# Top-k attention with an ELU feed-forward: four heads in the step of the last queries, another layout of the last keys, another schedule for the weights' decoding and the feed-forward

## The chip, the core and the metric

The kernel runs on one core of one Trainium2 chip. The metric is the device time in microseconds of one execution; the time before is the median of three runs. The profile is one further execution, recorded by the hardware profiler. Engines are named as in the profile: PE (TensorE matmul), PEld (its weight loads), DVE (VectorE), ACT (ScalarE), POOL (GpSimd), SP (the queue that issues the DMAs).

## The reference

Eight batches of eight heads, 576 tokens, 64 dimensions a head. The attention keeps, in every row of scores, those at or above the 32nd largest:

```python
def _attn_ref(q, k, v):
    B, H, S, D = q.shape                      # 8, 8, 576, 64
    scores = np.matmul(q, k.transpose(0, 1, 3, 2)) / np.sqrt(D)
    kth = np.partition(scores, -32, axis=-1)[..., -32:-31]
    scores = np.where(scores >= kth, scores, -1e9)
    attn = np.exp(scores - np.max(scores, axis=-1, keepdims=True))
    attn = attn / (np.sum(attn, axis=-1, keepdims=True) + 1e-9)
    return np.matmul(attn, v)

x = attn_out.transpose(0, 2, 1, 3).reshape(B * S, H * D)     # 4608 x 512
h = x @ w_in                                                # 512 x 2048
g = np.where(h > 0, h, np.exp(np.minimum(h, 0)) - 1)
out = g @ w_out                                             # 2048 x 512
```

The weights arrive as 64-bit floats and are turned into 32-bit floats on the chip. All arithmetic is in 32-bit floats.

## The kernel before

The 576 queries of a batch are four tiles of 128 (`qt` 0 to 3; tile `qt` holds every fourth token) and a rest of 64 (`qt` 4). A **step** is one query tile for one pair of heads `hp`: it computes two score tiles of 128 x 576 (`scores`, L252 and L261), finds the 32 largest of every row for each head (`select`: a MAX8, then three times a MATCH_REPLACE8 and a MAX8, L277, L281 and L287), turns the scores into exponentials that are zero outside the selection (`mask`, L298 to L302), divides by the sum (`normalise`, L309 to L313), transposes the result (`trans` and `trans_rest`, L326 to L342) and, once a group of one or two query tiles is complete, multiplies by V (`attend`, L360). L377 copies the product to `xT`, the transposed input of the feed-forward. In a step of the rest the two heads' 64 rows share the 128 partitions, so one selection serves both (`nh` = 1, `weight` = 0.5). There are 128 full steps and 32 of the rest.

The feed-forward works on **blocks** of one to three slots of 128 tokens. The first pair of batches has blocks of 1, 1, 2, 2 and 3 slots, each of the other three pairs has three blocks of 3: fourteen blocks, 36 slots. The last slot of a pair holds the rests of both batches. A block that has all its columns of `xT` adds its pieces to the list `ffn` (`ffn_pieces`): sixteen `hidden(f)`, each of four matmuls over the 512 inputs (L390), two ACT instructions (L398, L399) and one on DVE that writes `gT` (L400), and then for every slot four `project` pieces of four matmuls (L411), with an eviction (L420) and stores to `out` after the fourth. In the profile every 32-bit matmul is two PE instructions, so a piece of either kind shows as x8; a transpose is one.

Buffers: `sc` 5, `wk` 2, `et` 2, `kv` 5 of each kind, `xT` 2, `gT` 2 halves; in PSUM one tile of four banks for the scores, two banks for transposes, V products (`ps_t`), and two for the feed-forward (`ps_f`). `gT` lives in a pool that is opened only when the last weight is decoded and the raw buffers are given back.

The weights come in 32 pieces (16 of `w_in`, 16 of `w_out`). `hook`, called eight times in a full step between the passes of `select`, decodes one piece: `convert_first` and `convert_last` have three DVE instructions (L151, L154, L164), four on ACT and two on POOL.

The loop runs over the steps. Iteration n writes down the scores of step n+2, the selection of step n, the masking of step n-1 and the transposes of step n-2, and four times calls `feed`, which has a credit of 8 units a step (4 in a step of the rest) and takes pieces from `ffn` while the credit pays for them:

```python
        credit[0] = min(credit[0] + FEED * share * u.weight, 2 * FEED)
        while ffn and credit[0] >= ffn[0][0]:
```

What is left in `ffn` after the loop is written out at its end. The loads and transposes of the next batch's K, Q and V are put at fixed steps ahead of it (`at`). The source order is not the order in which an engine runs its instructions: the framework, which also sets all semaphores, arranges the instructions of each engine when the kernel is built. A tile taken from a pool waits until an older tile of the pool has had its last reader.

Of the kernel before, what the change touches and what calls it, by code (L numbers as in the profile page):

```python
# [16 lines left out]
EPS = 1.0e-9  # L17
STEEP = 1.0e30
FEED = 8.0
# [17 lines left out]
class Block:  # L37


    def __init__(self, slots):  # L40
        self.slots = slots
        self.xT = None
        self.gT = []
        self.left = 0
        self.tiles = [[] for _ in range(slots)]
# [10 lines left out]
class Step:  # L56


    def __init__(self, t, hp, group, at):
        self.t, self.hp = t, hp  # L60
        self.group, self.at = group, at
        self.nh = 1 if t.rem else 2
        self.weight = 0.5 if t.rem else 1.0
# [3 lines left out]
def kernel(  # L67
# [44 lines left out]
    rawpool = raws.enter_context(tc.tile_pool(name="raw", bufs=4))  # L112
# [13 lines left out]
    def weight(i):  # L126
        per = dff // WN
        if i < NC * per:
            c, f = divmod(i, per)
            src = moe_w_in[c * P : (c + 1) * P, 2 * f * WN : 2 * (f + 1) * WN]  # L130
            return src, w_in[:, c, f * WN : (f + 1) * WN]
        f = i - NC * per
        return moe_w_out[f * P : (f + 1) * P, :], w_out[:, f, :]
# [36 lines left out]
    decode = []  # L170

# [9 lines left out]
    def decode_piece(i):  # L181
        if i < 2 * NF:
            if i + 3 < 2 * NF:
                load_weight(i + 3)
            convert_first(i)
        if i > 0:
            convert_last(i - 1)

    loaded, kqT, vT = {}, {}, {}

# [14 lines left out]
    def load_v(b, hp):  # L205
        t = kvpool.tile([P, 2, J + 1, D], FP32, tag="vT", name="vT")
        for hh in range(2):
            h = 2 * hp + hh
            nc.sync.dma_start(
                t[:, hh, 0:J, :],  # L210
                v[b, h, 0:JP, :].rearrange("(p j) d -> p j d", j=J),
            )
        nc.sync.dma_start(
            t[0:R, :, J, :],
            v[b, 2 * hp : 2 * hp + 2, JP:S, :].rearrange("h p d -> p h d"),
        )
        vT[b, hp] = t

    def transpose_qk(b, hp):
        d = kvpool.tile([P, 2, S], FP32, tag="kqT", name="kqT")  # L220
        kqT[b, hp] = d
        srcs = [loaded.pop((b, hp, name)) for name in ("k", "q")]
        for i, src in enumerate(srcs):
            ps = ps_t.tile([P, JP], FP32, tag="t", name="qkps")
            for c in range(J):
                nc.tensor.transpose(
                    ps[:, c * P : (c + 1) * P],
                    src[:, c, :, :].rearrange("p h d -> p (h d)"),
                    ident[:],
                )  # L230
# [8 lines left out]
        nc.scalar.copy(  # L239
            d[:, :, JP:S], ps[:, 0 : 2 * R].rearrange("p (a s) -> p a s", a=2)  # L240
        )

    def scores(u):
        t = u.t
        kq = kqT[t.b, u.hp]
        q0 = t.qt * P
        u.sc = scpool.tile([P, 2, S], FP32, tag="sc", name="sc")
        ps = ps_sc.tile([P, 2, 2, 512], FP32, tag="s", name="scps")
        for half in range(2):
            for i in range(2):  # L250
                rows = slice(i * D, i * D + R) if t.rem else slice(0, P)
                nc.tensor.matmul(  # L252
                    ps[rows, i, half, 0:HS],
                    kq[i * D : (i + 1) * D, 1, q0 : q0 + t.ql],
                    kq[i * D : (i + 1) * D, 0, half * HS : (half + 1) * HS],
                    start=True,
                    stop=True,
                )
        for i in range(2):
            rows = slice(i * D, i * D + R) if t.rem else slice(0, P)  # L260
            nc.scalar.activation(  # L261
                u.sc[rows, 0 if t.rem else i, :].rearrange("p (a s) -> p a s", a=2),
                ps[rows, i, :, 0:HS],
                AF.Copy,
                scale=scale,
            )

    def select(u, i):
        if i >= u.nh:
            return  # L270
# [5 lines left out]
        hook()  # L276
# [3 lines left out]
        for r in range(TOP_K // 8 - 1):  # L280
# [7 lines left out]
            hook()  # L288

    def mask(u, i):  # L290

        if i >= u.nh:
            return
        if i == 0:
            u.den = small.tile([P, 2], FP32, tag="den", name="den")
        sc, low, top = u.sc[:, i, :], u.last[:, i, 7:8], u.first[:, i, 0:1]
# [9 lines left out]
    def normalise(u):  # L306
        nh = u.nh
        den = small.tile([P, 2], FP32, tag="dene", name="dene")
        nc.gpsimd.tensor_scalar_add(den[:, 0:nh], u.den[:, 0:nh], EPS)  # L309
        rec = small.tile([P, 2], FP32, tag="rec", name="rec")  # L310
        nc.vector.reciprocal(rec[:, 0:nh], den[:, 0:nh])  # L311
        for i in range(nh):
# [4 lines left out]
    def trans(u):  # L317

        g = u.group
        if g.et is None:  # L320
            n = len(g.tiles)
            g.et = etpool.tile([P, 2 * J + 2, n, P], FP32, tag="et", name="et")
        for i in range(u.nh):
            ps = ps_t.tile([P, JP], FP32, tag="t", name="eps")
            for c in range(J):
                nc.tensor.transpose(  # L326
                    ps[:, c * P : (c + 1) * P],
                    u.sc[:, i, c * P : (c + 1) * P],
                    ident[:],
                )  # L330
            nc.scalar.copy(  # L331
                g.et[:, i * J : (i + 1) * J, u.at, :],
                ps[:].rearrange("p (c q) -> p c q", c=J),
            )

    def trans_rest(u):

        g = u.group
        ps = ps_t.tile([P, JP], FP32, tag="t", name="eps")
        for i in range(u.nh):  # L340
            nc.tensor.transpose(ps[0:R, i * P : (i + 1) * P], u.sc[:, i, JP:S], ident[:])
        nc.scalar.copy(  # L342
            g.et[0:R, 2 * J : 2 * J + u.nh, u.at, :],
            ps[0:R, 0 : u.nh * P].rearrange("p (c q) -> p c q", c=u.nh),
        )

    def attend(g):
        t, hp = g.tiles[0], g.hp
        et, vt = g.et, vT[t.b, hp]
        n = sum(x.ql for x in g.tiles)  # L350
        ps = ps_t.tile([P, JP], FP32, tag="t", name="avps")
        for c in range(J + 1):
            for i in range(2):
                keys = slice(0, P if c < J else R)
                if t.rem:
                    w = et[keys, 2 * J if c == J else c, 0, i * R : (i + 1) * R]
                else:
                    w = et[keys, 2 * J + i if c == J else i * J + c, :, :]
                    w = w.rearrange("p a q -> p (a q)")
                nc.tensor.matmul(  # L360
                    ps[i * D : (i + 1) * D, 0:n],
                    vt[keys, i, c, :],
                    w,
                    start=(c == 0),
                    stop=(c == J),
                )
        c0 = 0
        tiles = list(g.tiles)
        while tiles:
            blk, lo = tiles[0].block, tiles[0].cols.start  # L370
            c1 = c0
            while tiles and tiles[0].block is blk:
                blk.left -= 1
                c1 += tiles.pop(0).ql
            if blk.xT is None:
                blk.xT = xtpool.tile([P, NC, T], FP32, tag="xT", name="xT")
            nc.scalar.copy(blk.xT[:, hp, lo : lo + c1 - c0], ps[:, c0:c1])  # L377
            c0 = c1
            if blk.left == 0:
                ffn.extend(ffn_pieces(blk))  # L380

    def ffn_pieces(blk):
        n_tok = blk.slots * P

        def hidden(f):
            if f % NG == 0:
                blk.gT.append(late["g"].tile([P, NG, T], FP32, tag="g", name="gT"))
# [18 lines left out]
        def project(s, part):  # L406
# [18 lines left out]
        return [(blk.slots, lambda f=f: hidden(f)) for f in range(NF)] + [  # L425
            (3.8, lambda s=s, part=part: project(s, part))
# [6 lines left out]
    blocks = []  # L433
    for b in range(B):
        if b % 2 == 0:
            sizes = (1, 1, 2, 2, 3) if b == 0 else (3, 3, 3)
            slots = [(x, s) for x in map(Block, sizes) for s in range(x.slots)]
# [15 lines left out]
        for qts in ((0,), (1,), (2, 3), (4,)) if b == 0 else ((0, 1), (2, 3), (4,)):  # L453
            for hp in range(NHP):
# [9 lines left out]
    for b in range(1, B):  # L464
        f = first[b]
        for hp, (ahead, ready, late_v) in enumerate(
            ((12, 9, 8), (9, 5, 0), (6, 4, -1), (5, 3, -2))
# [5 lines left out]
    credit = [0.0]  # L473

    def feed(u, share):

        if "g" not in late:
            return
        credit[0] = min(credit[0] + FEED * share * u.weight, 2 * FEED)
        while ffn and credit[0] >= ffn[0][0]:  # L480
            cost, piece = ffn.pop(0)
            credit[0] -= cost
            piece()

    load_qk(0, 0)
    for i in range(3):
# [18 lines left out]
    closing = []  # L505
    for n in range(NS + 3):
        for fn, args in todo.pop(n, []):
            fn(*args)
        now = steps[min(n, NS - 1)]
# [5 lines left out]
        feed(now, 0.25)  # L515
        if cur:
            select(cur, 0)
        while closing:
            attend(closing.pop())
        feed(now, 0.25)  # L520
        if prev:
            mask(prev, 1)
        if done:
            trans(done)
        feed(now, 0.25)
# [4 lines left out]
        if done:  # L530
            trans_rest(done)
            if done.at == len(done.group.tiles) - 1:
                closing.append(done.group)
        feed(now, 0.25)
    while ffn:
        ffn.pop(0)[1]()
# [33 lines left out]
```

## Time and profile before

| | us |
|---|---|
| median of three runs | 1917.54 (1917.00 to 1917.82) |
| the profiled execution | 1917.18 |
| its span, first to last instruction | 1915.4 |
| PE busy / DVE busy / ACT busy / POOL busy | 1709.2 / 1615.8 / 1169.8 / 447.2 |
| mean granted TensorE clock | 0.948 of full speed |
| PE busy in 48 to 96 us, 96 to 144 us | 0.0, 10.8 |
| last matmul of attention / last matmul | 1815 / 1911 |

A page row of the costliest groups gives line, engine, operation, tiles written and read, shape, count, then busy time, the mean of one in ns, and the engine's idle time just before. Busy time is a union: neighbours that overlap in the pipeline count once, so busy over count is below the mean. In a timeline a row is start, length, engine, line, operation, tiles, shape and count, and in brackets the engine's idle time before it with what ended it.

### The profile page before, as it was taken

To read this page: it belongs to the slowest core of one execution; us is meant where nothing else is said; L and a number is where in the kernel's file an instruction comes from. 1 tells how busy PE (TensorE), PEld (TensorE's weight loads), DVE (VectorE), ACT (ScalarE), POOL (GpSimd) and SP (SyncE) were. 2 spreads that over 40 slices of the span, in tenths; PEclk is the share of its full clock that TensorE was granted. 3 is DMA by queue.
4 is the path that set the end of the run, shared out by engine and by line. 5 is a ranking of instruction groups with operands and counts; after the bars stand their busy time and mean duration, and the time that the engine had idled before them with its cause. 6 is when DMAs were issued, how large, how long until landed. Compare 5 with 4: busy or idle time off the path is not lost.

```text
span 1915.4 us, 24954 instructions
## 1 busy us (share of the span) xinstructions
PE 1709.2 (89%) x7984; PEld 946.7 (49%) x7984; DVE 1615.8 (84%) x3360; ACT 1169.8 (61%) x2453; POOL 447.2 (23%) x1096
## 2 busy tenths in 40 slices
PE   4028999999999999899989999999999999999999
PEld 2015656465554455455454455455555455445553
DVE  7999989999799998996999777997899777999310
ACT  6677667576666776575566466566566566557330
POOL 4774212222122222221222111221122211222000
PEclk7557999999899999999999999999999999999999
DMA  6430011000200110001100010000100000000000
GB/s 175 150 130 3 19 31 32 18 13 19 56 1 12 38 31 19 12 13 43 37 1 6 24 44 19 12 18 19 49 13 0 25 19 19 7 12 1 12 6 17
DMA packets 100610, 56.14 MB, mean 29 GB/s; under 512 B 83584, under 2 KB 91776, under 8 KB 100480
## 3 DMA queue, kind: packets, MB, share of 16 engines
q1 hardware_dynamic: 100480, 54.55, 10.3%
q8 instruction: 64, 1.05, 0.2%
q14 instruction: 66, 0.54, 0.1%
HBM read 45.09 MB, written 9.44 MB: 28 GB/s over the span
## 4 chain that ended last, share of the span: by engine, by line
DVE 56%; PE 31%; ACT 8%; issue 2%; POOL 1%; DMA 1%; SPq 0%; POOLq 0%; ACTq 0%; DVEq 0%
DVE wk L281 22%; DVE m L287 20%; PE hps L390 11%; PE ops L411 8%; DVE m L277 7%; PE scps L252 5%; PE avps L360 3%; DVE gT L400 3%; ACT sc L301 2%; PE eps L326 2%; ACT sc L261 2%; ACT sc L302 1%; DVE raw L164 1%; DVE raw L154 1%; DVE raw L151 1%
## 5 line engine op out<-in xcount | busy, mean ns | idle before, releaser
L287 DVE MAX8 m<-wk 128x8 f32<-128x576 f32 x864 | 631.9, 761 | 4.1
L390 PE MATMUL hps<-xT,w_in 128*128 128x384 f32 (+2 forms) x1792 | 544.5, 451 | 16.3 <-DVE gT L400 15.2
L411 PE MATMUL ops<-w_out,gT 128*128 128x512 f32 x1152 | 534.2, 604 | 0.0
L281 DVE MATCH_REPLACE8 wk<-m,wk 128x576 f32<-128x576 f32 x576 | 432.4, 754 | 0.0
L301 ACT ACTIVATE sc<-sc,neg 128x576 f32<-128x576 f32 x288 | 223.1, 775 | 336.5 <-POOL neg L298 336.0
L390 PEld LDWEIGHTS hps<-xT,w_in 128*128 128x128 f32 x1792 | 310.9, 192 | 196.0 <-DVE gT L400 31.0
L411 PEld LDWEIGHTS ops<-w_out,gT 128*128 128x128 f32 x1152 | 208.7, 192 | 223.1 <-issue 219.1
L252 PE MATMUL scps<-kqT 64*128 64x288 f32 (+1 forms) x1280 | 255.4, 456 | 17.4 <-ACT sc L261 15.8
L298 POOL TENSOR_SCALAR neg<-m 128x1 f32<-128x1 f32 x288 | 62.8, 218 | 847.2 <-DVE m L287 845.9
L277 DVE MAX8 m<-sc 128x8 f32<-128x576 f32 x288 | 215.7, 758 | 51.9 <-ACT sc L261 51.5
L313 POOL TENSOR_SCALAR sc<-sc,rec 128x576 f32<-128x576 f32 x288 | 214.0, 753 | 116.6 <-DVE rec L311 93.3
L302 ACT ACTIVATE sc<-sc,gap 128x576 f32<-128x576 f32 x288 | 223.4, 776 | 15.4 <-ACT sc L301 1.5
L360 PE MATMUL avps<-et,vT 128*64 128x256 f32 (+5 forms) x2000 | 205.9, 342 | 26.3 <-ACT et L342 25.6
L281 DVE MATCH_REPLACE8 wk<-m,sc 128x576 f32<-128x576 f32 x288 | 216.6, 754 | 0.0
L326 PE MATMUL eps<-ident,sc 128*128 128x128 f32 x1152 | 173.2, 284 | 48.1 <-ACT xT L377 23.5
L261 ACT ACTIVATE sc<-scps 128x576 f32<-128x576 f32 (+1 forms) x320 | 192.6, 641 | 28.9 <-PE scps L252 27.7
L400 DVE SCALAR_TENSOR_TENSOR gT<-n,hps 128x384 f32<-128x384 f32 (+2 forms) x224 | 109.9, 491 | 116.7 <-ACT n L399 115.0
L326 PEld LDWEIGHTS eps<-ident,sc 128*128 128x128 f32 x1152 | 133.4, 145 | 124.5 <-issue 70.7
L331 ACT COPY et<-eps 128x512 f32<-128x512 f32 x288 | 159.9, 585 | 51.4 <-PE eps L326 50.5
L360 PEld LDWEIGHTS avps<-et,vT 128*64 128x64 f32 (+1 forms) x2000 | 113.7, 141 | 135.2 <-issue 48.2
L252 PEld LDWEIGHTS scps<-kqT 64*128 64x128 f32 (+1 forms) x1280 | 121.0, 186 | 104.3 <-issue 58.2
L398 ACT ACTIVATE n<-hps 128x384 f32<-128x384 f32 (+2 forms) x224 | 98.3, 439 | 119.7 <-PE hps L390 118.1
(41 smaller groups left out, 969.1 us busy)
## 6 DMA issues: line engine op xcount, KB each, us to landing
kin<-in_k_dram SPq DMA_DIRECT2D x64, 128.0 KB, 2.7
qin<-in_q_dram SPq DMA_DIRECT2D x64, 128.0 KB, 2.8
raw<-in_moe_w_in_dram SPq DMA_DIRECT2D x16, 512.0 KB, 4.6
vT<-in_v_dram SPq DMA_DIRECT2D x64, 128.0 KB, 2.1
raw<-in_moe_w_out_dram SPq DMA_DIRECT2D x16, 512.0 KB, 3.2
out_dram<-osb SPq DMA_DIRECT2D x32, 256.0 KB, 2.3
kin<-in_k_dram SPq DMA_DIRECT2D x32, 32.0 KB, 2.5
qin<-in_q_dram SPq DMA_DIRECT2D x32, 32.0 KB, 2.5
```

The costliest lines, as they stand in the source:

```text
L252: nc.tensor.matmul(ps[rows, i, half, 0:HS], kq[i * D : (i + 1) * D, 1, q0 : q0 + t.ql], kq[i * D : (i + 1) * D, 0, half * HS : (half + 1) ...
L261: nc.scalar.activation(u.sc[rows, 0 if t.rem else i, :].rearrange("p (a s) -> p a s", a=2), ps[rows, i, :, 0:HS], AF.Copy, scale=scale,)
L277: nc.vector.max(m, sc)
L281: nc.vector.match_replace(wk[:], m, cur, TAKEN)
L287: nc.vector.max(m, cur)
L301: nc.scalar.activation(sc, sc, AF.Prelu, bias=neg[:], alpha=STEEP)
L302: nc.scalar.activation(sc, sc, AF.Exp, bias=gap[:], accum_out=u.den[:, i : i + 1])
L313: nc.gpsimd.tensor_scalar(u.sc[:, i, :], u.sc[:, i, :], rec[:, i : i + 1], 1.0, ALU.mult, ALU.mult)
L326: nc.tensor.transpose(ps[:, c * P : (c + 1) * P], u.sc[:, i, c * P : (c + 1) * P], ident[:],)
L360: nc.tensor.matmul(ps[i * D : (i + 1) * D, 0:n], vt[keys, i, c, :], w, start=(c == 0), stop=(c == J),)
L390: nc.tensor.matmul(ps[:, 0:n_tok], w_in[:, i, f * P : (f + 1) * P], blk.xT[:, i, 0:n_tok], start=(i == 0), stop=(i == NC - 1),)
L411: nc.tensor.matmul(blk.o[:], blk.gT[f // NG][:, f % NG, s * P : (s + 1) * P], w_out[:, f, :], start=(f == 0), stop=(f == NF - 1),)
```

## The change

- A step of the rest now takes the last queries of **four** heads (two on each half of the partitions, two selections): 16 such steps in place of 32. `weight` and `nh` go. `attend` serves two head pairs in such a group.
- The scores of a head are two matmuls, of 512 and of 64 keys. Head 1's 64 last keys stand ahead of its others in `sc`, so that both heads' last keys are side by side and the transposes go in nine chunks of 128 (`turn`: four, one and four) instead of eight and two halves. V's last keys lie on partitions 0 to 63 for one head and 64 to 127 for the other, with a DMA each.
- `hook` is called twice in a selection instead of four times. The raw buffers are three (before: four), and a pool `early` holds the `gT` of block 0. `w_in` is decoded by columns first.
- In the first eight steps the masking, division and transposes are written one iteration earlier.
- `feed` compares a running sum of TensorE time, spent by attention and feed-forward, with a budget of 12.4 us a step, and asks of every piece that enough weight pieces are decoded.
- The loads and transposes of the next batch stand at other steps.

The core of the diff:

```diff
-FEED = 8.0
+PACE = 12.4
...
     def __init__(self, t, hp, group, at):
-        self.nh = 1 if t.rem else 2
-        self.weight = 0.5 if t.rem else 1.0
+        self.masked = self.normal = self.turned = False
+        if t.rem:
+            rows = [(4 * hp, 0), (4 * hp + 2, 0), (4 * hp + 3, 1), (4 * hp + 1, 1)]
+            self.heads = [
+                (h, i, slice(64 * (n % 2), 64 * (n % 2) + 64))
+                for n, (h, i) in enumerate(rows)
+            ]
+        else:
+            self.heads = [(2 * hp + i, i, slice(0, 128)) for i in range(2)]
...
-    rawpool = raws.enter_context(tc.tile_pool(name="raw", bufs=4))
+    early = raws.enter_context(tc.tile_pool(name="early", bufs=1))
+    rawpool = raws.enter_context(tc.tile_pool(name="raw", bufs=3))
...
-            c, f = divmod(i, per)
+            f, c = divmod(i, NC)
...
+    decoded = [0]
...
     def decode_piece(i):
         if i < 2 * NF:
-            if i + 3 < 2 * NF:
-                load_weight(i + 3)
+            if i + 2 < 2 * NF:
+                load_weight(i + 2)
             convert_first(i)
         if i > 0:
             convert_last(i - 1)
+            decoded[0] = i
...
     def scores(u):
+        first = (0, 3 * JP - R)
+        main = (0, 3 * JP)
+        rest = (JP, 3 * JP - R)
+        for start, keys in ((main, slice(0, JP)), (rest, slice(JP, S))):
+            for h, i, rows in u.heads:
+                kq = kqT[u.t.b, h // 2]
+                part = slice(i * D, (i + 1) * D)
                 nc.tensor.matmul(
+                    ps[rows, start[i] : start[i] + keys.stop - keys.start],
+                    kq[part, 1, q0 : q0 + u.t.ql],
+                    kq[part, 0, keys],
...
+        spent(1.2)
...
     def select(u, i):
-        hook()
         nc.vector.max(m, sc)
...
             nc.vector.max(m, cur)
-            hook()
+            if r != 1:
+                hook()
...
+    def turn(u, chunks):
...
+        sc = u.sc[:, :, :].rearrange("p i s -> p (i s)")
+        for c in range(n):
+            c0 = (chunks.start + c) * P
+            nc.tensor.transpose(ps[:, c * P : (c + 1) * P], sc[:, c0 : c0 + P], ident[:])
+        spent(0.115 * n)
...
         def hidden(f):
-            if f % NG == 0:
-                blk.gT.append(late["g"].tile([P, NG, T], FP32, tag="g", name="gT"))
+            if f == 0 and blk.number == 0:
+                g = early.tile([P, NF, P], FP32, tag="g", name="gT")
+                blk.gT = [g[:, 0:NG], g[:, NG:NF]]
+            elif f % NG == 0 and blk.number > 0:
+                g = late["g"].tile([P, NG, T], FP32, tag="g", name="gT")
+                blk.gT.append(g[:])
...
-        return [(blk.slots, lambda f=f: hidden(f)) for f in range(NF)] + [
-            (3.8, lambda s=s, part=part: project(s, part))
+        part = {1: 1.15, 2: 1.85, 3: 2.7}[blk.slots]
+        behind = 2 * NF + 1 if blk.number else 0
+        return [
+            (part, max(behind, NC * (f // 4 + 1)), lambda f=f: hidden(f))
+            for f in range(NF)
+        ] + [
+            (3.55, max(behind, NF + (part + 1) * NF // 4),
+             lambda s=s, part=part: project(s, part))
             for s in range(blk.slots)
             for part in range(4)
         ]
...
-            for hp in range(NHP):
+            for hp in range(NHP // 2 if qts == (4,) else NHP):
...
-            ((12, 9, 8), (9, 5, 0), (6, 4, -1), (5, 3, -2))
+            ((8, 6, 5), (6, 4, 0), (4, 3, -1), (3, 2, -2))
...
-        if "g" not in late:
-            return
-        credit[0] = min(credit[0] + FEED * share * u.weight, 2 * FEED)
-        while ffn and credit[0] >= ffn[0][0]:
-            cost, piece = ffn.pop(0)
-            credit[0] -= cost
-            piece()
+        clock["due"] += PACE * share
+        while ffn and decoded[0] >= ffn[0][1] and (
+            clock["spent"] + 0.5 * ffn[0][0] <= clock["due"]
+        ):
+            cost, _, piece = ffn.pop(0)
+            clock["spent"] += cost
+            piece()
+        clock["spent"] = max(clock["spent"], clock["due"] - PACE)
...
+        if n < TIGHT:
+            while closing:
+                attend(closing.pop(0))
+            feed(0.5)
+            select(cur, 0)
+            mask(cur, 0)
+            if prev:
+                normalise(prev)
+                turn(prev, slice(0, J))
+                turn(prev, slice(J, J + 1))
+                turn(prev, slice(J + 1, 2 * J + 1))
+            feed(0.5)
+            select(cur, 1)
+            mask(cur, 1)
+            continue
...
     while ffn:
-        ffn.pop(0)[1]()
+        ffn.pop(0)[2]()
```

The line that makes the decoding list is the same in both kernels: `decode += [lambda i=i: decode_piece(i) for i in range(2 * NF + 1)]`; `NF` is 16 and `NC` is 4.

More of the change, by code (lines that the diff above doesn't have):

```diff
@@ L37, with __init__ @@
 class Block:
-    def __init__(self, slots):
-        self.slots = slots
+    def __init__(self, number, slots):
+        self.number, self.slots = number, slots
         self.xT = None
@@ L187, in decode_piece, with spent @@
             convert_last(i - 1)
+            decoded[0] = i
     loaded, kqT, vT = {}, {}, {}
+    def spent(cost):
+        clock["spent"] += cost
     def load_qk(b, hp):
@@ L205, in load_v @@
     def load_v(b, hp):
[L206 removed]
+        t = kvpool.tile([P, 2 * J + 1, D], FP32, tag="vT", name="vT")
         for hh in range(2):
@@ L209, in load_v @@
             nc.sync.dma_start(
-                t[:, hh, 0:J, :],
+                t[:, hh * J : (hh + 1) * J, :],
                 v[b, h, 0:JP, :].rearrange("(p j) d -> p j d", j=J),
             )
[L213 to L216, printed above, removed]
+            nc.sync.dma_start(t[hh * R : (hh + 1) * R, 2 * J, :], v[b, h, JP:S, :])
         vT[b, hp] = t
@@ L241, in transpose_qk @@
         )
+        spent(1.6)
     def scores(u):
-        t = u.t
-        kq = kqT[t.b, u.hp]
-        q0 = t.qt * P
+        q0 = u.t.qt * P
         u.sc = scpool.tile([P, 2, S], FP32, tag="sc", name="sc")
[L248 to L251, printed above, removed]
+        ps = ps_sc.tile([P, 4 * JP], FP32, tag="s", name="scps")
+        first = (0, 3 * JP - R)
[5 more added lines that the diff above has]
+                part = slice(i * D, (i + 1) * D)
                 nc.tensor.matmul(
-                    ps[rows, i, half, 0:HS],
-                    kq[i * D : (i + 1) * D, 1, q0 : q0 + t.ql],
-                    kq[i * D : (i + 1) * D, 0, half * HS : (half + 1) * HS],
+                    ps[rows, start[i] : start[i] + keys.stop - keys.start],
+                    kq[part, 1, q0 : q0 + u.t.ql],
+                    kq[part, 0, keys],
                     start=True,
@@ L258, in scores @@
                 )
+        spent(1.2)
         for i in range(2):
-            rows = slice(i * D, i * D + R) if t.rem else slice(0, P)
             nc.scalar.activation(
[L262 to L265, printed above, removed]
+                u.sc[:, i, :], ps[:, first[i] : first[i] + S], AF.Copy, scale=scale
             )
     def select(u, i):
-        if i >= u.nh:
-            return
         if i == 0:
@@ L287, in select @@
             nc.vector.max(m, cur)
-            hook()
+            if r != 1:
+                hook()
     def mask(u, i):
-        if i >= u.nh:
+        if u.masked:
             return
@@ L295, in mask @@
             u.den = small.tile([P, 2], FP32, tag="den", name="den")
+        u.masked = i == 1
         sc, low, top = u.sc[:, i, :], u.last[:, i, 7:8], u.first[:, i, 0:1]
@@ L306, in normalise @@
     def normalise(u):
-        nh = u.nh
+        if u.normal:
+            return
+        u.normal = True
         den = small.tile([P, 2], FP32, tag="dene", name="dene")
-        nc.gpsimd.tensor_scalar_add(den[:, 0:nh], u.den[:, 0:nh], EPS)
+        nc.gpsimd.tensor_scalar_add(den[:], u.den[:], EPS)
         rec = small.tile([P, 2], FP32, tag="rec", name="rec")
-        nc.vector.reciprocal(rec[:, 0:nh], den[:, 0:nh])
-        for i in range(nh):
+        nc.vector.reciprocal(rec[:], den[:])
+        for i in range(2):
             nc.gpsimd.tensor_scalar(
@@ L315, in normalise @@
             )
-    def trans(u):
+    def turn(u, chunks):
+        if u.turned:
+            return
         g = u.group
         if g.et is None:
[L321 to L334, printed above, removed]
@@ L336, in trans_rest @@
-    def trans_rest(u):
-        g = u.group
-        ps = ps_t.tile([P, JP], FP32, tag="t", name="eps")
-        for i in range(u.nh):
-            nc.tensor.transpose(ps[0:R, i * P : (i + 1) * P], u.sc[:, i, JP:S], ident[:])
+            g.et = etpool.tile([P, 2 * J + 1, len(g.tiles), P], FP32, tag="et", name="et")
+        ps = ps_t.tile([P, JP], FP32, tag="t", name="eps")
+        sc = u.sc[:, :, :].rearrange("p i s -> p (i s)")
+        n = chunks.stop - chunks.start
+        for c in range(n):
+            c0 = (chunks.start + c) * P
+            nc.tensor.transpose(ps[:, c * P : (c + 1) * P], sc[:, c0 : c0 + P], ident[:])
@@ L342, in trans_rest @@
+        spent(0.115 * n)
         nc.scalar.copy(
-            g.et[0:R, 2 * J : 2 * J + u.nh, u.at, :],
-            ps[0:R, 0 : u.nh * P].rearrange("p (c q) -> p c q", c=u.nh),
-        )
+            g.et[:, chunks, u.at, :],
+            ps[:, 0 : n * P].rearrange("p (c q) -> p c q", c=n),
+        )
+        if chunks.stop == 2 * J + 1:
+            u.turned = True
+            if u.at == len(g.tiles) - 1:
+                closing.append(g)
     def attend(g):
-        t, hp = g.tiles[0], g.hp
@@ L349, in attend @@
-        et, vt = g.et, vT[t.b, hp]
-        n = sum(x.ql for x in g.tiles)
+        t = g.tiles[0]
         ps = ps_t.tile([P, JP], FP32, tag="t", name="avps")
[L352 to L366, printed above, removed]
+        n = P if t.rem else sum(x.ql for x in g.tiles)
@@ new lines, in attend @@
+        for k in range(2 if t.rem else 1):
+            hp = 2 * g.hp + k if t.rem else g.hp
+            vt = vT[t.b, hp]
+            for c in range(J + 1):
+                for i in range(2):
+                    rows = slice(0, P) if c < J else slice(i * R, (i + 1) * R)
+                    chunk = J if c == J else i * (J + 1) + c
+                    w = g.et[rows, chunk, :, :].rearrange("p a q -> p (a q)")
+                    cols = slice(0, n)
+                    if t.rem:
+                        c0 = R * (k if i == 0 else 1 - k)
+                        w = w[:, c0 : c0 + R]
+                        cols = slice(k * R, (k + 1) * R)
+                    nc.tensor.matmul(
+                        ps[i * D : (i + 1) * D, cols],
+                        vt[rows, 2 * J if c == J else i * J + c, :],
+                        w,
+                        start=(c == 0),
+                        stop=(c == J),
+                    )
@@ L367, in attend @@
+        spent(1.5 if n == P else 2.5)
+        if t.rem:
+            finish(t.block, 2, slice(2 * g.hp, 2 * g.hp + 2), t.cols,
+                   ps[:, 0:n].rearrange("p (a q) -> p a q", a=2))
+            return
         c0 = 0
@@ L369, in attend, with finish @@
         while tiles:
-            blk, lo = tiles[0].block, tiles[0].cols.start
-            c1 = c0
+            blk, lo, parts = tiles[0].block, tiles[0].cols.start, 0
             while tiles and tiles[0].block is blk:
[L373 to L380, printed above, removed]
+                parts += 1
+                hi = tiles.pop(0).cols.stop
+            finish(blk, parts, g.hp, slice(lo, hi), ps[:, c0 : c0 + hi - lo])
+            c0 += hi - lo
+    def finish(blk, parts, at, cols, src):
+        if blk.xT is None:
+            blk.xT = xtpool.tile([P, NC, T], FP32, tag="xT", name="xT")
+        nc.scalar.copy(blk.xT[:, at, cols], src)
+        blk.left -= parts
+        if blk.left == 0:
+            ffn.extend(ffn_pieces(blk))
     def ffn_pieces(blk):
@@ L432 @@
     steps, first = [], {}
-    blocks = []
+    number = 0
     for b in range(B):
@@ L436 @@
             sizes = (1, 1, 2, 2, 3) if b == 0 else (3, 3, 3)
-            slots = [(x, s) for x in map(Block, sizes) for s in range(x.slots)]
+            slots = []
+            for x in sizes:
+                blk = Block(number, x)
+                number += 1
+                slots += [(blk, s) for s in range(x)]
         first[b] = len(steps)
@@ L471, with feed @@
             at(f - late_v, load_v, b, hp)
-    credit = [0.0]
-    def feed(u, share):
-        if "g" not in late:
-            return
-        credit[0] = min(credit[0] + FEED * share * u.weight, 2 * FEED)
-        while ffn and credit[0] >= ffn[0][0]:
-            cost, piece = ffn.pop(0)
-            credit[0] -= cost
+    clock = {"spent": 0.0, "due": 0.0}
+    def feed(share):
+        clock["due"] += PACE * share
[3 more added lines that the diff above has]
+            cost, _, piece = ffn.pop(0)
+            clock["spent"] += cost
             piece()
+        clock["spent"] = max(clock["spent"], clock["due"] - PACE)
     load_qk(0, 0)
-    for i in range(3):
+    for i in range(2):
         load_weight(i)
@@ L505 @@
     closing = []
+    TIGHT = 2 * NHP
     for n in range(NS + 3):
@@ L508 @@
             fn(*args)
-        now = steps[min(n, NS - 1)]
         ahead, cur, prev, done = step(n + 2), step(n), step(n - 1), step(n - 2)
@@ L512 @@
             scores(ahead)
+        if n < TIGHT:
[13 more added lines that the diff above has]
+            continue
         if prev:
             mask(prev, 0)
-        feed(now, 0.25)
+        feed(0.25)
         if cur:
@@ L518 @@
         while closing:
-            attend(closing.pop())
-        feed(now, 0.25)
+            attend(closing.pop(0))
+        feed(0.25)
         if prev:
@@ L523 @@
         if done:
-            trans(done)
-        feed(now, 0.25)
+            turn(done, slice(0, J))
+            turn(done, slice(J, J + 1))
+        feed(0.25)
         if cur:
@@ L530 @@
         if done:
[L531 to L534, printed above, removed]
+            turn(done, slice(J + 1, 2 * J + 1))
+        feed(0.25)
     while ffn:
-        ffn.pop(0)[1]()
+        ffn.pop(0)[2]()
 _INS = ['q', 'k', 'v', 'moe_w_in', 'moe_w_out']
```

## The prediction, made before the changed kernel was run

> **What bounds the kernel now.** I read the page's engine shares first, then the table of stretches, then timelines of single steps. The page has
>
> ```profile
> PE 1709.2 (89%) x7984; PEld 946.7 (49%) x7984; DVE 1615.8 (84%) x3360; ACT 1169.8 (61%) x2453; POOL 447.2 (23%) x1096
> ```
>
> so two engines are nearly full, and which one limits depends on the stage. The table of stretches (columns: stretch, length, then busy us and instruction count of PE, PEld, DVE, ACT, POOL, then granted clock) for one pair of batches:
>
> ```profile
> 811.50:1256.70 445.20, 418.44 (x1915) 225.37 (x1914) 385.16 (x808) 270.18 (x564) 88.52 (x256) 0.98 0.08 22
> ```
>
> 445 us a pair, PE at 94%, DVE at 87%: TensorE sets the pace there. The hidden pieces (L390) hold 136 us of PE in this stretch and the projections (L411) 134 us; attention has the other 148. Where PE keeps up, VectorE sets it:
>
> ```profile
> 344.58 0.23 POOL L309 TENSOR_SCALAR dene<-den 128x2 f32<-128x2 f32 x1 [1.71 <-ACT sc L302]
> 345.02 1.42 DVE L287 MAX8 m<-wk 128x8 f32<-128x576 f32 x2
> 346.41 0.76 DVE L281 MATCH_REPLACE8 wk<-m,wk 128x576 f32<-128x576 f32 x1
> 347.13 0.76 DVE L281 MATCH_REPLACE8 wk<-m,wk 128x576 f32<-128x576 f32 x1
> 347.79 1.43 DVE L287 MAX8 m<-wk 128x8 f32<-128x576 f32 x2
> 349.12 0.17 DVE L311 RECIPROCAL rec<-dene 128x2 f32<-128x2 f32 x1
> 349.18 0.76 DVE L277 MAX8 m<-sc 128x8 f32<-128x576 f32 x1
> ```
>
> Two things are to be seen. A full step (two heads, fourteen passes) takes 9.7 us: its first MAX8 starts at 339.49, the next step's at 349.18, without a gap. And the order on VectorE is not the source's: the two heads' chains alternate. The reciprocal had its input at 344.81 and ran only at 349.12, when a chain had ended, since in the source it stands behind both selects of its step. The same holds for a whole step: scores evicted by 1192.30 wait for their first MAX8 until 1205.25, while the earlier step's two chains run:
>
> ```profile
> 1191.13 1.17 ACT L261 ACTIVATE sc<-scps 128x576 f32<-128x576 f32 x2
> 1200.36 0.76 DVE L277 MAX8 m<-sc 128x8 f32<-128x576 f32 x1
> 1205.25 0.76 DVE L277 MAX8 m<-sc 128x8 f32<-128x576 f32 x1
> ```
>
> I read this as a rule of the build: each engine takes, of what is ready, what comes first in the source, and two live chains leave no opening. The last view is the wait that couples both halves, the two xT buffers:
>
> ```profile
> 1164.87 10.59 PE L390 MATMUL hps<-xT,w_in 128*128 128x384 f32 x32 [1.07 <-DVE gT L400]
> 1175.50 0.33 ACT L377 COPY xT<-avps 128x64 f32<-128x64 f32 x2 [1.53 <-PE hps L390]
> 1178.12 1.42 DVE L277 MAX8 m<-sc 128x8 f32<-128x576 f32 x2 [0.75 <-ACT sc L261]
> ```
>
> Attention cannot write the next block's xT until the last hidden matmul of an older block has read it; VectorE's selection restarts 2.6 us after that.
>
> **What the Trainium skill says.** "PSUM — Partial Sum Buffer", section "Engine vs sequencer instructions", calls the VectorE queue strict FIFO: what is placed late stays late, as the reciprocal's 4.3 us show. "TensorEngine Tiling (Array Packing)", section "Tiling Modes", lets different tiles of the array work in parallel; the trace agrees: four score matmuls of 288 columns take 1.24 us, where at the hidden layer's dense rate (2.58 us for four of 384) they would take 1.94. "TensorE: Matmul & The Clock Gate", section on the HAM clock gate, halves the clock after about 3.4 us of idleness; here the granted clock is 0.50 from 144 to 156 us and 1.00 from 172.
>
> **The change part by part.**
>
> *The gate.* The new feed() releases a piece only if decoded[0] has reached its second entry. decode_piece(i) sets decoded[0] = i, and i runs over range(2 * NF + 1), so it ends at 2 * NF = 32. Every block but number 0 asks for `behind` = 2 * NF + 1 = 33. So in the loop only block 0 is fed; the pieces of blocks 1 to 13 (35 of 36 slots) are written by the last `while ffn`, behind all attention. By the rule above they still start early where an engine has nothing else ready. On PE they find room: attention takes some 4.1 us of a 9.7 us step (148 / 36), and projections need no VectorE until their eviction on ACT. On DVE gT (L400) now stands behind every select of every later step, and two chains are always live. The queue behind it: two hidden pieces fill both ps_f banks and wait, no further piece can start, xT is not freed, and after at most five sc buffers the attention stops for it. Only then gT runs. Selection and hidden layer become serial.
>
> The sum on VectorE's path:
> - First MAX8 at 14.8 us, as before.
> - 144 steps of 9.7 = 1396.8. The number of selects stays 288 (the 32 half steps become 16 full ones), so nothing is saved but 16 reciprocals of 0.16.
> - Decode, L151, L154 and L164: 27.6 + 34.9 + 30.3 = 92.8, only spread over twice as many selects.
> - Block 0's gT: 16 x 0.28 = 4.5. Sum: 1509.
> - Eleven blocks (1 to 11) must free xT before attention can go on. Of each 16 pieces two are already in ps_f. A dense piece takes 1.98 / 2 = 0.99 us for one slot, 9.00 / 5 = 1.80 for two, 41.3 / 16 = 2.58 for three (the PE records at 173, 300 and 1828 us): 14 x (0.99 + 2 x 1.80 + 8 x 2.58) = 353.
> - Restart after each: 11 x 2.6 = 29. PE has been idle before it while VectorE used up its ready steps, so the first 4 us run at half clock: about 2 us each, 22, an estimate.
>
> Selection ends at 1913. Then block 12's other 14 hidden pieces, 36.1, and its 12 projection pieces at 41.2 / 12 = 3.43, 41.2; then block 13 as in the tail before, 1915.4 - 1828.1 = 87.3. Span 2078; the profiled run was 1.8 us longer than its span (1917.18, which is the median less 0.4): **2080 us**.
>
> *Four heads to a step.* Scores of two heads of one row half now differ in column group: at best 1.2 us less per pair of half steps, 16 x 1.2 = 19 of PE; at worst nothing. Evictions fall by 32 x 0.645 = 21 us of ACT. All lies beside VectorE's path: worth 0 here. If PE bounds again it counts in full. The two V remainders become two DMAs: 32 more issues of 0.33 us on SP over the whole span: 0, at worst a few us where an issue stands in front of a load that is waited for.
>
> *Last keys side by side.* Nine transposes and one 128-column copy replace ten and a 256-column one: 1.04 + 0.38 against about 1.17 of PE per step, 0.25 x 128 = 32, plus 11 for the half steps: hidden by VectorE, 0 here. The copy order in sc (head 1's last keys first) costs nothing.
>
> *Two pieces per select, three raw buffers, w_in by columns.* A raw load now waits for the buffer of piece i-1 and has some 10 us until piece i+2; loads land in 4.6. So 0; if each came late by 1 us, +30. *Block 0 early*: its 33 us of PE move into the first 200 us, where PE idles; since PE is not the bound, worth 0.
>
> *Loads and transposes of the next batch* come at other steps, of about the same lead in time: 0, at worst some us at seven batch borders.
>
> **The rivals.** (a) *The gate opens, or gT finds its turns.* Then PE is the bound as now, with 33 us moved to the front and 19 + 43 less work: 1917 - 33 - 62 = 1822. VectorE would allow it: 1616 busy and an 87 us tail give 1718. Against it stand the two constants 32 and 33 in the code and the reciprocal's wait. (b) *gT slips in at chain ends.* Each piece that does so saves 2.58 less its own 0.55, so 2.0 us. 163 us separate my sum from the time before, so 80 of the 154 gT in it would have to slip in, about one in two steps, to break even; beyond that the change is faster. A quarter of them gives 2000. For it: first MAX8s do enter when a chain ends. Against: it is then the next step's MAX8, ready 13 us, that is ahead of gT. (c) *Stalls cost more*: each restart needs transposes, scores and eviction at a cold clock, with batch borders on top; 5 us more each is 2135.
>
> **How the numbers follow.** Serial selection and hidden layer, with (c): 0.72. Partly slipped in, still slower: 0.09. At the old time: 0.03. Faster, (a) or the far end of (b): 0.16. About 0.2% is what a measurement here can tell from no change. Slower 0.81, same 0.03, faster 0.16. The range runs from a partial slip-in, 1940, to (c), 2140; the likeliest case alone is 2040 to 2140.
>
> **What would show it.** Right: gT at a median wait of many us behind its L399; stretches of 30 to 40 us in which VectorE does nothing but gT, PE at hidden pieces throughout, each ended by an xT copy; steps at 9.7 us between them with PE under 60% once projections are done; blocks 12 and 13 after the last select, 160 us of pure PE. Wrong: gT between the selects of ordinary steps, or a pair period at or under 445 us.

## The result, and the profile after

The changed kernel takes 2128.11 us (median of four runs, 2126.22 to 2128.56) against 1917.27 us before: a ratio of 1.1104, 95% interval 1.1084 to 1.1123. It is slower by 211 us. The forecast was 2080 us, range 1940 to 2140. The profiled execution has a span of 2125.8 us.

The engine shares of its page, and from the page's forty slices (busy tenths, 53 us each) the rows of TensorE and VectorE:

```profile
PE 1798.3 (85%) x7840; PEld 987.0 (46%) x7840; DVE 1580.1 (74%) x3344; ACT 1153.7 (54%) x2389; POOL 440.1 (21%) x1080
PE   5577738997398999996399999997489999997999
DVE  7999997599969483999949392999939584797110
```

The same two rows of the kernel before (48 us a slice):

```profile
PE   4028999999999999899989999999999999999999
DVE  7999989999799998996999777997899777999310
```

VectorE is busy for 36 us less than before, TensorE for 89 us more, with 144 instructions fewer. Most of that rise goes with the order of the work and with a lower mean clock (0.894 against 0.948): the kernel before with its feed-forward written last, the second experiment below, has unchanged instructions and is busy on TensorE for 1772.2 us, 63 more, at 0.884. The rest belongs to other parts of the change and comes up again below. The two engines now take turns. Ahead of the tail VectorE's row falls to 2 to 5 tenths and comes back to 9, again and again; TensorE's row has hollows of its own (7 3, 6 3, 4) just ahead of three of VectorE's. In the kernel before no slice between start and tail fell under 6.

Between the hollows a step is as fast as it was in the best stretches before. A timeline of VectorE (start, length, engine, line, operation):

```profile
1440.11 0.14 DVE L327 RECIPROCAL rec<-dene 128x2 f32<-128x2 f32 x1
1440.17 0.74 DVE L289 MAX8 m<-sc 128x8 f32<-128x576 f32 x1
1440.83 0.07 DVE L293 MATCH_VALUE_LOAD wk<-m,wk 128x8 f32 x1
1440.89 0.74 DVE L293 MATCH_REPLACE8 wk<-m,wk 128x576 f32<-128x576 f32 x1
...
1449.88 0.74 DVE L289 MAX8 m<-sc 128x8 f32<-128x576 f32 x1
```

The first maxima (L289) of the two successive steps are 9.7 us apart, without a gap and without a gT (L425 now) between them. Once the weights are decoded, the steps' starts, read off the same line over the whole trace, are 9.7 us apart nearly everywhere, except for eleven of 31.6 to 65.7 us, each with exactly sixteen gT in it. What a gT waits for meanwhile is shown by two pieces of block 9, in timelines of ACT, VectorE and PE:

```profile
1446.88 0.54 ACT L424 ACTIVATE n<-n 128x384 f32<-128x384 f32 x1
1447.83 0.52 ACT L424 ACTIVATE n<-n 128x384 f32<-128x384 f32 x1
...
1546.88 0.53 DVE L425 SCALAR_TENSOR_TENSOR gT<-n,hps 128x384 f32<-128x384 f32 x1
1548.06 0.55 DVE L425 SCALAR_TENSOR_TENSOR gT<-n,hps 128x384 f32<-128x384 f32 x1
...
1547.47 12.91 PE L415 MATMUL hps<-xT,w_in 128*128 128x384 f32 x32 [27.97 <-DVE gT L425]
```

Both inputs were ready by 1448.35, and both gT ran about 100 us later. In between VectorE did ten steps. The two pieces held both ps_f banks, no third could start, and TensorE, out of other work, stood idle for 28 us until the first of the two gT had run. The table of stretches (stretch, length, then busy us and instruction count of PE, PEld, DVE, ACT, POOL, then granted clock) gives both halves of the alternation:

```profile
1512.00:1536.00 24.00, 6.82 (x32) 3.23 (x32) 24.00 (x54) 9.45 (x18) 5.06 (x15) 0.57 0.00 1
1560.00:1584.00 24.00, 24.00 (x76) 14.15 (x75) 4.99 (x9) 9.48 (x19) 0.00 (x0) 1.00 0.00 1
```

First VectorE is full and TensorE busy for 6.8 of 24 us, at a granted clock of 0.57; later TensorE is full and VectorE does nothing but nine gT. The longest pause, from timelines of PE, ACT and DVE:

```profile
1761.61 19.48 PE L436 MATMUL ops<-w_out,gT 128*128 128x512 f32 x45
1780.92 41.44 PE L415 MATMUL hps<-xT,w_in 128*128 128x384 f32 x128
...
1822.40 0.43 ACT L398 COPY xT<-avps 128x128 f32<-128x128 f32 x2 [1.53 <-PE hps L415]
...
1826.28 1.42 DVE L289 MAX8 m<-sc 128x8 f32<-128x576 f32 x2 [1.90 <-ACT sc L279]
```

It holds the last projections of the block ahead, all sixteen hidden pieces in one run (128 instructions), then at once the copy into xT that had waited, and 3.9 us later the next selection. In the table of waits (us in total, times, longest) two entries have grown from 115.0 and 15.2 us in the kernel before: VectorE's wait for a gT's input, in the pauses, and TensorE's wait for a gT, ahead of them:

```profile
DVE gT L425 <- ACT n L424: 427.8, 195, 43.2
PE hps L415 <- DVE gT L425: 134.0, 9, 28.5
```

### The profile page after: what moved, and what is told of

It reads as the page before. It is cut to its first block, busy times and chain, and to the rows that moved or that the text cites. A ratio compares the mean times of both kernels' runs of the same rounds, so it can differ in the third digit from the quotient of the medians.

```text
span 2125.8 us, 24553 instructions
## 1 busy us (share of the span) xinstructions
PE 1798.3 (85%) x7840; PEld 987.0 (46%) x7840; DVE 1580.1 (74%) x3344; ACT 1153.7 (54%) x2389; POOL 440.1 (21%) x1080
## 4 chain that ended last, share of the span: by engine, by line
DVE 50%; PE 45%; ACT 2%; DMA 2%; issue 1%; POOL 1%; SPq 0%; POOLq 0%; DVEq 0%; ACTq 0%
PE hps L415 22%; DVE wk L293 22%; DVE m L299 19%; PE ops L436 14%; DVE m L289 6%; PE scps L270 3%; PE eps L345 2%; PE avps L373 2%; DMA raw<-in_moe_w_in_dram 1%; DVE raw L167 1%; DVE raw L164 1%; DVE raw L177 1%; DMA raw<-in_moe_w_out_dram 1%; PE qkps L241 0%; ACT sc L279 0%
## 5 line engine op out<-in xcount | busy, mean ns | idle before, releaser
L415 PE MATMUL hps<-xT,w_in 128*128 128x384 f32 (+2 forms) x1792 | 530.5, 457 | 134.4 <-DVE gT L425 134.0
L299 DVE MAX8 m<-wk 128x8 f32<-128x576 f32 x864 | 613.3, 748 | 0.6
L415 PEld LDWEIGHTS hps<-xT,w_in 128*128 128x128 f32 x1792 | 334.3, 199 | 323.4 <-DVE gT L425 138.9
L425 DVE SCALAR_TENSOR_TENSOR gT<-n,hps 128x384 f32<-128x384 f32 (+2 forms) x224 | 111.0, 496 | 427.9 <-ACT n L424 427.8
L345 PE MATMUL eps<-ident,sc 128*128 128x128 f32 x1296 | 241.4, 309 | 102.3 <-POOL sc L329 74.3
L270 PE MATMUL scps<-kqT 64*128 64x512 f32 (+3 forms) x1280 | 285.2, 485 | 49.3 <-ACT sc L279 48.6
L345 PEld LDWEIGHTS eps<-ident,sc 128*128 128x128 f32 x1296 | 162.8, 154 | 266.9 <-POOL sc L329 116.9
L347 ACT COPY et<-eps 128x512 f32<-128x512 f32 (+1 forms) x432 | 195.3, 480 | 117.0 <-PE eps L345 116.3
L373 PE MATMUL avps<-et,vT 128*64 128x256 f32 (+5 forms) x2000 | 239.2, 369 | 17.9 <-ACT et L347 15.9
L289 DVE MAX8 m<-sc 128x8 f32<-128x576 f32 x288 | 213.2, 744 | 23.4 <-ACT sc L279 23.4
L373 PEld LDWEIGHTS avps<-et,vT 128*64 128x64 f32 (+1 forms) x2000 | 133.4, 156 | 117.8 <-issue 43.2
L279 ACT ACTIVATE sc<-scps 128x576 f32<-128x576 f32 x288 | 174.8, 650 | 10.9 <-PE scps L270 10.9
```

Of the source, the lines that this page charges most:

```text
L270: nc.tensor.matmul(ps[rows, start[i] : start[i] + keys.stop - keys.start], kq[part, 1, q0 : q0 + u.t.ql], kq[part, 0, keys], start=True, s ...
L289: nc.vector.max(m, sc)
L299: nc.vector.max(m, cur)
L345: nc.tensor.transpose(ps[:, c * P : (c + 1) * P], sc[:, c0 : c0 + P], ident[:])
L347: nc.scalar.copy(g.et[:, chunks, u.at, :], ps[:, 0 : n * P].rearrange("p (c q) -> p c q", c=n),)
L373: nc.tensor.matmul(ps[i * D : (i + 1) * D, cols], vt[rows, 2 * J if c == J else i * J + c, :], w, start=(c == 0), stop=(c == J),)
```

## The experiments

The theory: the gate (32 against 33) keeps blocks 1 to 13 out of the loop, therefore gT stands behind all selections on VectorE, and through ps_f and xT the hidden layer and the selection become serial. The main rival: another part of the change (steps of four heads, the key layout, slower decoding) costs the time. A second: two xT buffers are too few. All ratios are against the kernel before, on the same chip.

**The gate opened.**

```diff
-        behind = 2 * NF + 1 if blk.number else 0
+        behind = 2 * NF if blk.number else 0
```

> The changed kernel with `behind = 2 * NF` (32), a value that the counter reaches. Theory (the gate keeps blocks 1 to 13 out of the loop, so gT stands behind every selection and the hidden layer becomes serial with it): all eleven long pauses of VectorE go, TensorE bounds as in the kernel before, minus some 95 us of work moved or saved: 1822 us, between 1790 and 1870. Rival (steps of four heads, the new key layout or the slower decoding cost the time): it stays above 1917 us, and the pauses stay or turn into others.

Measured 1892.7 us, ratio 0.9865 (0.9847 to 0.9882). One digit is worth 235 us and turns the change into a gain of 1.3%; the rival is out. No pause with sixteen gT in it is left: no step is longer than 25 us after decoding. But it is 71 us above my 1822 and outside my range. One reason is on its page: TensorE is busy for 42 us more than in the kernel before (1709.2), at nearly the same clock (0.945 against 0.948), where the 1822 had counted on 62 us less. I come back to it below.

```profile
PE 1751.4 (93%) x7840; PEld 954.0 (50%) x7840; DVE 1591.0 (84%) x3344; ACT 1134.3 (60%) x2389; POOL 439.5 (23%) x1080
DVE  6999999999998989988887889988787898988410
```

**The feed-forward last, in the kernel before.**

```diff
-        if "g" not in late:
-            return
+        return
         credit[0] = min(credit[0] + FEED * share * u.weight, 2 * FEED)
```

> The kernel before with a feed() that returns at once, so that the whole feed-forward is written after the loop; nothing else of the change. Theory: the same eleven pauses of 30 to 66 us, one more for block 0, steps of 9.7 us between them: 2150 us, between 2110 and 2190. Rival (the loss comes from other parts of the change): below 1990 us.

Measured 2188.7 us in a single run, inside the expected range. There are twelve pauses of 30 to 70 us, each with sixteen gT. So the source position alone makes a loss of this kind and size, without any other part of the change. The slices of its VectorE show the same comb:

```profile
DVE  7999877599959363999949381999949572898110
```

**Three xT buffers.**

```diff
-    scpool = pool("sc", 5)
+    scpool = pool("sc", 4)
-    xtpool = pool("xt", 2)
+    xtpool = pool("xt", 3)
```

> The changed kernel with three xT buffers in place of two and four score buffers in place of five, which makes the room. Theory: the hidden layer stays serial with the selection wherever it is forced, so one more buffer only moves each pause later and one of them into the tail: 2128 us less at most the 12 us extra of three pauses and one restart, 2070 to 2135. Rival (two xT buffers are the cause, attention waits because it has no room): most pauses go, below 1980 us.

Measured 2151.0 us in a single run: not faster, so the number of xT buffers is not the cause, but also above my 2070 to 2135. (The score buffers, cut to four in the same edit, do not show: the steps between the pauses still take 9.7 us.) The trace shows why: ten pauses instead of eleven, and the selection ends some 60 us earlier, at 1891 us (the last step's first maximum at 1881.6, plus a step); but three blocks instead of two are left for the tail, 258 us instead of 175. I had moved only a hidden layer into the tail and forgotten the projections that come with it. With two buffers those ran under the selection.

**Only gT moved.**

```diff
-            nc.vector.scalar_tensor_tensor(
-                out=blk.gT[f // NG][:, f % NG, 0:n_tok],
+            with tc.high_priority():
+                nc.vector.scalar_tensor_tensor(
+                    out=blk.gT[f // NG][:, f % NG, 0:n_tok],
...
```

> The changed kernel with its gate as it is: all pieces of blocks 1 to 13 are still written after the loop, only their one VectorE instruction each (gT) is given high priority in the build. Theory (what is lost is gT's turn on VectorE alone, PE and ACT have room for late pieces): 1840 us, between 1800 and 1900. Rival (matmuls and ACT instructions written last starve as well, or the budget feed is needed): above 2000 us.

Measured 1846.5 us, ratio 0.9629 (0.9608 to 0.9651). The gate stays shut, every matmul and ACT instruction of the blocks stays written last, and 282 us go. What was lost was one instruction's turn on VectorE. Its timeline has the gT between the passes, where the changed kernel has none:

```profile
1290.80 1.41 DVE L299 MAX8 m<-wk 128x8 f32<-128x576 f32 x2
1292.12 0.54 DVE L426 SCALAR_TENSOR_TENSOR gT<-n,hps 128x384 f32<-128x384 f32 x1
1292.58 0.09 DVE L293 MATCH_VALUE_LOAD wk<-m,wk 128x8 f32 x1
1292.65 0.74 DVE L293 MATCH_REPLACE8 wk<-m,wk 128x576 f32<-128x576 f32 x1
1293.31 0.16 DVE L327 RECIPROCAL rec<-dene 128x2 f32<-128x2 f32 x1
```

and TensorE, which finds its late pieces by itself, fills all but the start:

```profile
PE   5567899999999999999999999999999999999999
DVE  6999999989999999999999955999999872997010
```

This is the fastest of all versions here. Two pauses of 65 us remain on VectorE (the 5 5 in its row, and the last 7 2): TensorE is full in them, with projections and then a hidden layer that xT waits for. There TensorE is the bound.

**gT first in the kernel before.** The same edit, alone.

> The kernel before with gT given high priority in the build, nothing else. In its own order gT starts at a median 0.14 us (mean 0.40) after its input, so it is not starved there. Theory: no gain to be had, 1917 us within 1%. Rival (gT first is worth some 70 us anywhere, and the 1846 us say nothing on the change): below 1880 us.

Measured 1914.8 us, ratio 0.9991 (0.9982 to 0.9999): nothing. In the order of the kernel before gT was not late, and moving it is no gain as such.

**Gate opened and gT first.**

> The changed kernel with the gate open (32) and gT first: the budget feed of 12.4 us a step stays, gT's turn is certain. Theory A (the 46 us between the open gate at 1893 and gT first at 1846 are gT's waits, mean 0.47 us against 0.21): 1850 us. Theory B (they are the budget, which places pieces ahead of attention and so holds the attention back; with gT first alone late pieces only fill gaps): 1880 to 1900 us, as with the gate open.

Measured 1876.4 us, ratio 0.9799 (0.9771 to 0.9828): between the two theories, below both of B's ends and 26 us above A. gT's turn explains some 16 of the 46 us between the open gate and gT first (a rough figure, since the runs here spread from 1873 to 1887); the other 30 go with the budget feed. The trace is consistent with theory B for these: the last step starts its first maximum at 1741 us with the budget and at 1679 without it. They are idle time of TensorE: its busy time is nearly the same, 1724.7 us with the budget and 1728.6 without, in spans of 1871.3 and 1843.3. What makes that idle time was not tried.

**The order alone, without the rest of the change.** The kernel before, feed-forward last and gT first.

> The kernel before with the feed-forward written after the loop and gT first: what order alone gives, without the change's other parts. Theory (the parts that I priced at 0 beside VectorE count once TensorE bounds: 33 us of block 0 moved to the front, about 60 us of PE work saved): 1846 + 93 = 1939 us, at least 1900. Rival (they are worth little): 1846 to 1870 us.

Measured 1893.5 us, ratio 0.9875 (0.986 to 0.989). Against the 2188.7 us of the feed-forward last without it, the edit of gT is worth 295 us here, as it was worth 282 in the changed kernel. On the sum of the parts neither theory holds: order alone gives 23 us, and the other parts 47, half of the 93 that I had added up.

**Two decoded pieces per selection, in the kernel before.**

```diff
-        hook()
         nc.vector.max(m, sc)
...
-            hook()
+            if r != 1:
+                hook()
```

> The kernel before with two decoded pieces per selection in place of four, at the same places as in the changed kernel; the feed-forward still waits until all are decoded. It shows whether the shorter VectorE decoding of the changed kernel (L164, L167, L177 at means of 670, 784 and 872 ns against 862, 1092 and 946 before) comes from spreading it. Theory: yes, the three lines fall together by 15 us or more, step 9 starts at about 177 us instead of 190; but the feed-forward begins some 40 us later and TensorE bounds, so 1930 to 1960 us. Rival: the means stay, they came from something else; then step 9 starts at about 190.

Measured 1905.8 us, ratio 0.9945 (0.9927 to 0.9962): faster by 0.6%, where I had expected 13 to 43 us slower. The step numbered 9 starts at 170.8 us instead of 189.7. The three decoding lines together fall from 92.8 to 82.5 us, less than the 15 I asked for, and unevenly: L154 from 1092 to 742 ns, L164 from 946 to 842, L151 up from 862 to 997. The feed-forward's start, which I had put 40 us later, does not move: the last weight is done at 172.5 us instead of 157.4, but the first gT runs at 173.5 and ran at 173.2 before. So the selection is 19 us further on when the feed-forward begins. That this lead makes the gain of 11 us is likely, but was not tried.

**gT first, block 0 late.** The version at 1846.5 with block 0 treated as the others.

```diff
-            if f == 0 and blk.number == 0:
+            if False:
...
-        behind = 2 * NF + 1 if blk.number else 0
+        behind = 2 * NF + 1
```

> The changed kernel with gT first as in the run at 1846 us, and block 0 treated as the others: behind the gate, with its gT in the late pool, so not before the last decoding. Theory: its 33 us of TensorE work leave the idle first 200 us and TensorE bounds, so 1846 + 33 = 1879 us, 1865 to 1890. Rival (early block 0 is worth nothing, the gain over 1893 us is all saved PE work): 1840 to 1855 us.

Measured 1871.2 us, ratio 0.9761 (0.9745 to 0.9777), as the theory said: early block 0 is worth 25 us where TensorE bounds. With the runs before it the gain of 70 us splits, in this order of the steps: order 23 (1916.6 to 1893.5), steps of four heads with key layout, decoding and loads 22 (to 1871.2), early block 0 25 (to 1846.5).

## Why the prediction held, point by point

**The gate** was read rightly, and the experiments with one digit and with one instruction's priority show it. Reading the counter's last value against the constant decided the sign; the diff's own description would have led to rival (a), 1822 us, the wrong side.

**The sum** came out 48 us short in span (2078 against 2125.8), from three terms:

| term | predicted, us | measured, us |
|---|---|---|
| start of the step numbered 9 (8 decoded steps and one more behind it) | 14.8 + 9 x 9.7 + 92.8 + 4.5 = 199 | 177.1 |
| a step between pauses | 9.7 | 9.7 |
| eleven pauses and restarts | 353 + 29 + 22 = 404 | 463 |
| after the selection | 165 | 175 |

- The pauses were mis-sized. Measured they are the eleven long steps, 582.5 us together, less 9.7 each and less 1.2 each that the following step (8.5 us) gives back. The failing step is "of each 16 pieces two are already in ps_f". That holds for blocks 1, 2, 3, 4, 6 and 9, whose first two gT waited 5 to 117 us. For blocks 5, 7, 8, 10 and 11 the projections of the block ahead still held TensorE, and no piece was ready: all sixteen ran in the pause, 5 x 5.2 = 26 us. Three of them (5, 8 and 11) were preceded by projections inside the pause too, like the one shown above; these steps take 65.7 us against about 53 for a pause of the same block size without it, 13 each, of which the two missing pieces are 5. Both together are 50 of the 59 us.
- The start was over-sized by 22 us. I took the decoding lines' busy time from the kernel before, where they are slower: 92.8 us there, 74.4 in the changed kernel. The step of the prediction that failed is "92.8, only spread"; it became cheaper. The spread is one part of that: half the hooks in the kernel before gave 82.5. Early block 0 seems to be another: with gT first the same three lines take 72.6, and 81.8 with block 0 late. The 4 us that are left of the 22 were not traced.
- The tail was 10 us longer than 36.1 + 41.2 + 87.3. Attention's last transposes and V products run between block 12's first hidden pieces, 8 us of TensorE that the sum had left out.

So the forecast's closeness is in part luck: a start 22 us too long hides more than a third of the 59 us that the pauses lacked. Rival (c) gave 2135, still closer to the measured 2128, but by dearer restarts, which are not what was missing.

**The parts priced at 0** beside VectorE's path could be priced at 0 only there. Where TensorE bounds again, early block 0 counts 25 us (I had 33), and all the rest together 22 where I had 62 for PE work alone. That price was wrong in its sign. These are the pages of the order alone and of gT first with block 0 late, which differ by these parts, at mean clocks of 0.954 and 0.956:

```profile
PE 1707.1 (90%) x7984; PEld 932.0 (49%) x7984; DVE 1594.6 (84%) x3360; ACT 1185.3 (63%) x2453; POOL 445.6 (24%) x1096
PE 1732.7 (93%) x7840; PEld 931.4 (50%) x7840; DVE 1577.8 (84%) x3344; ACT 1140.8 (61%) x2389; POOL 440.2 (24%) x1080
```

TensorE is busy for 26 us more. Its transposes take 20 us less (245.8 to 225.6; I had 43 less), but its scores take 15 more (241.2 to 256.6; I had 19 less), and its V products, which I had left out, 28 more (197.5 to 225.4). The 22 us are gained because TensorE's idle time falls by 47, from 185 to 138 us. Which part of the change does that was not separated; the gain of 11 us from half the hooks hints at the decoding.

**Rivals (b) and (c)**: after step 8 no gT slipped in ahead of the pauses, except the two of a waiting pair in the last 3 us of a selection, so (b) fell altogether; of (c), the restarts were near their price, 3.9 us in the pause shown against 2.6.

**The signs to look for**: pauses with nothing but gT, their end at an xT copy, 9.7 us between them, TensorE under 60% in some stretches and 175 us of TensorE after the last select were all there. One was wrong: the median wait of gT is 0.03 us, not many. Only the two pieces in ps_f can wait; all others cannot even start, and run undisturbed once the pause has come. 17 of 224 waited over 2 us.

The Trainium skill's strict FIFO ("PSUM — Partial Sum Buffer", "Engine vs sequencer instructions") agrees with gT's 100 us behind ten steps: ready as it was, it ran only where the build had put it. The skill's clock gate ("TensorE: Matmul & The Clock Gate", the HAM clock gate) agrees with the granted 0.57 in the stretch shown where TensorE mostly idles and 1.00 in the later one where it is full.

## What to carry to other kernels

Where the builder takes on each engine what comes first in the source, background work starves on the engine that the foreground keeps full, however little of it there is: look for the one instruction of the late work that needs that engine, and give it precedence; the rest may stand last and fill gaps by itself. When a gate compares a counter with a constant, work out the counter's last value before pricing anything else. A pause behind a shared buffer lasts as long as the whole backlog ahead of the release, so count what stands in that queue, not only the work that frees the buffer.

## What was not expected of the hardware

The integer decoding on VectorE got cheaper by being spread: mean durations of its three lines, 862, 1092 and 946 ns in the kernel before, are 670, 784 and 872 in the changed kernel for the same 128 x 512 operands. In the kernel before with half the hooks they are 997, 742 and 842, and in the changed kernel with gT first and block 0 late 722, 898 and 939. What else runs at the same moment seems to set them; which engine or transfer it is was not tried.
